# Row sums by float32 transposes, one spreading moved, and loads dealt out in a two-branch attention kernel with gradients

## The chip, the core and the metric

The kernel runs on one core of a Trainium2 chip. A core has five engines that run their own instruction queues: TensorE (matrix products and transposes into PSUM, the accumulators' memory), VectorE, ScalarE, GpSimd, and SyncE, which only issues DMAs. GpSimd and ScalarE issue DMAs too, in line with their other work. In the profile these are PE (with PEld for the loading of weights), DVE, ACT, POOL and SP. The metric is the device time of one execution, in microseconds (us).

## The reference

The forward pass mixes two branches token by token, `g * a + (1 - g) * b`, with a gate `g = sigmoid(sum(x * gate_w))`. There are 2048 tokens of width 576.

Branch a is attention with 32 query heads of width 18 and a single key and value head:

```python
q = (x @ wq).reshape(B, S, H, Dh).transpose(0, 2, 1, 3)
k = x @ wk
v = x @ wv
p = softmax(einsum('bhqd,bkd->bhqk', q, k) * Dh ** (-0.5))
a = einsum('bhqk,bkd->bhqd', p, v).transpose(0, 2, 1, 3).reshape(B, S, H * Dh) @ wo
```

Branch b goes through the tokens in 64 segments of 32, with 8 memory rows that each segment hands to the next:

```python
for s in range(n_seg):
    h = concatenate([mem, x[:, s * seg_len:(s + 1) * seg_len]], axis=1)
    q, k, v = (einsum('btd,dhe->bhte', h, W) for W in (Wq, Wk, Wv))
    scores = where(mask, einsum('bhqe,bhke->bhqk', q, k) * scale, -1e9)
    o = einsum('bhqk,bhke->bhqe', softmax(scores), v)
    o = einsum('bhte,hed->btd', o, Wo)
    mem = o[:, :M]
    outs.append(o[:, M:])
```

with 32 heads of width 128. The kernel returns the output and, for a given gradient of it, the gradients of `x`, of branch a's four weights, of the first memory, of branch b's four weights and of `gate_w`, twelve arrays in bfloat16.

## The kernel before

The program is one unrolled stream of instructions per engine; the order on each engine is the order in which the Python code writes it (most of it runs under a manual schedule). Its stages, one after another:

1. Preparation and the token projections of branch b.
2. The forward chain woven with pass 1 of branch a (from about 420 to 2147 us). The memory rows of branch b form a chain over 64 segments, `b_chain_fwd`; it yields 16 times a segment. `weave` takes one step of pass 1 (`a_pass1`, 1024 steps: the product `a_S`, its exponential `a_E`, the product `a_dP`, the elementwise `a_W`, the accumulations `a_acc`) and then one step of the chain, in turn. At the head of each segment but the first, the new memory rows are put together: the output projection of the segment before has left 32 x 4 partial rows in PSUM, VectorE has copied them to `c_hs` (line 565) and, masked, to `c_hx` (line 566), and `row_sums` adds the groups of rows and turns the result so that the model's width lies along the partitions: four float32 products with a 0/1 selector (`selp`, `sel8`). `put_rows` (line 322) copies the result to `hm`, the tile that the next projections load as weights. Helper lines 82 and 87 issue nearly all products and transposes.
3. The token stage `b_bulk` (from about 2160 to 2790 us): attention of the 2048 tokens of branch b, forward and backward, in 128 groups of 4 heads x 128 tokens. It is a pipeline written by hand: iteration `t` runs the stages of the list `order`, each for group `t - n`. `st_R` sums the exponentials of a row (`x_l`, line 816), takes the reciprocal (`x_r`) and lets GpSimd write `x_P`; `st_OT` transposes the attention output into the PSUM tile `x_tr`, of which there are two in turn, and VectorE copies it to `x_oT` (line 841); `st_VT` transposes `v` into the next `x_tr`; `st_T` and `st_DT` are VectorE transposes (`x_PT`, `x_DT`); `st_Y` is GpSimd's `x_Y` and `x_dS`. Four groups are one chunk, for which SyncE loads q, dO, k, v and the block-diagonal memory rows kB and vB; `after` says behind which stage of the chunk's last group each load for a later chunk is issued. Stores are collected in `due` and issued by `flush` at the end of a later iteration. q, dO and k have rings of four chunks; when the chunks run out, the same places load twelve weight tiles for the next stage.
4. The backward chain woven with pass 2 of branch a (from about 2814 to 4500 us): `b_chain_bwd`, 16 steps a segment, last segment first, each behind one step of `a_pass2` (`b_S`, `b_E`, `b_dP`, `b_dS`, `b_acc`). In 44 of the segments each segment also carries four units of other work, the memory rows' share of the keys' and values' gradients: `kv_load`, `kv_blk` (line 1085: GpSimd spreads a block of P or dS over four masked copies, `r_kb`), `kv_mm` (the products, into `r_x`) and `kv_out` (ScalarE copies to `r_kvo`, GpSimd issues the store, line 1109). `kv_mm(n)` also calls `kv_blk(n + 1)`. In the chain's own work, GpSimd copies `r_dS` into `r_dspad` (line 1039), VectorE transposes it to `r_dsq` (line 1043), GpSimd spreads that to `r_dSqB` (line 270), and TensorE uses it two steps later.
5. Post-processing, weight gradients and the final stage (from about 4500 us).

Of the kernel before, what the change touches and what calls it, by code (L numbers as in the profile page):

```python
# [10 lines left out]
ALU = mybir.AluOpType  # L11
AX = mybir.AxisListType
BF16 = mybir.dt.bfloat16
F32 = mybir.dt.float32
U16 = mybir.dt.uint16
U32 = mybir.dt.uint32
P = 128
# [3 lines left out]
NSL = 6  # L21
# [25 lines left out]
class Kern:  # L47
# [83 lines left out]
    def setup_B_consts(self, pool):  # L131
        nc = self.nc
# [40 lines left out]
        s8 = pool.tile([P, 8], F32, name="sel8")  # L173
        nc.gpsimd.memset(s8[:], 0.0)
        tm = pool.tile([P, 2, 32], BF16, name="tmask")
        nc.gpsimd.memset(tm[:], 0.0)
        sq = pool.tile([P, 2, 8], F32, name="selp")
        nc.gpsimd.memset(sq[:], 0.0)
        for c in range(4):
            nc.gpsimd.affine_select(out=s8[:], in_=s8[:], compare_op=ALU.not_equal, fill=1.0,  # L180
                                    base=-32 * c, pattern=[[-1, 8]], channel_multiplier=1)
            nc.gpsimd.affine_select(out=sq[:, c % 2, :], in_=sq[:, c % 2, :], compare_op=ALU.not_equal, fill=1.0,
                                    base=-32 * c, pattern=[[-1, 8]], channel_multiplier=1)
            nc.gpsimd.memset(tm[32 * c:32 * c + 32, c % 2, :], 1.0)
        self.sel8, self.selp = s8, sq
# [129 lines left out]
    def row_sums(self, pm, hs, hx):  # L315
        for k in range(2):
            self.mm(pm[:, 0:4, :].rearrange("p (f k) q -> p k f q", k=2)[:, k], lhsT=hs[:, k, :], rhs=self.selp[:])
        for j in range(2):
            self.mm(pm[:, 4 + j, :], lhsT=hx[:].rearrange("p a b -> p (a b)")[:, 64 - 64 * j:192 - 64 * j], rhs=self.sel8[:])

    def put_rows(self, t, pm):
        self.nc.vector.tensor_copy(t[:, :, 0:8], pm[:])
# [18 lines left out]
    def b_chain_fwd(self, keep, sp, psum):  # L341
# [69 lines left out]
        for s in range(NSEG):  # L411
# [43 lines left out]
            if s:  # L455
                pm = psum.tile([P, NSL, 8], F32, name="c_pj", bufs=1)
                self.row_sums(pm, hs, hx)
                self.put_rows(h_, pm)
# [208 lines left out]
    def b_bulk(self, wp, vp, kp, sp, psum):  # L667
# [65 lines left out]
        def flush(end=False):  # L733
            for dst, src in due.pop(0):
                (nc.scalar if end else nc.sync).dma_start(dst, src)
            due.append([])
# [169 lines left out]
        def st_KE(t):  # L906
# [3 lines left out]
            if t % 4 == 3:  # L910
                c2 = t // 4 % 2
                for i in range(4):
# [3 lines left out]
        order = [(2, st_M), (0, st_QT), (None, mem_T), (5, st_B0), (0, st_KT), (2, st_R), (4, st_Y), (5, st_B1), (4, st_OT),  # L916
                 (2, st_GT), (3, st_T), (5, st_DT), (3, st_Om), (5, st_Qm), (2, st_VT), (1, st_Sm), (3, st_Dm), (1, st_S),
                 (5, st_K), (3, st_D), (5, st_KE), (3, st_O), (5, st_Q)]
        after = {st_O: ("vB", "v"), st_D: ("mT",), st_KE: ("q", "dO"), st_Q: ("k", "kB")}
# [7 lines left out]
        for t in range(NG + 6):  # L927
            sc["D"] = psum.tile([P, 512], F32, name="x_D", bufs=1)
            sc["Sb"] = psum.tile([P, 512], F32, name="x_S", bufs=1)
            for n, st in order:  # L930
                if n is None:
                    st(t)
                    continue
                if 0 <= t - n < NG:
                    st(t - n)
                if st in after and t - n >= 0 and (t - n) % 4 == 3:
                    c = (t - n) // 4
                    for w in after[st]:
                        load(c + (BQ if w in deep else 3 if w in ("mT", "v") else 2), (w,))
            if t % 4 == 2 and t // 4 - 2 in range(NTT // 4):  # L940
                self.dl_rows(t // 4 - 2, sp, psum)
            flush(t >= NG)
        flush(True)
# [51 lines left out]
    def b_chain_bwd(self, wot, sp, kd, kvp, keep, psum):  # L995
# [93 lines left out]
        def kv_mm(n):  # L1089
# [10 lines left out]
            kv_blk(n + 1)  # L1100
# [19 lines left out]
        for s in reversed(range(NSEG)):  # L1120
# [81 lines left out]
            kv_mm(n0)  # L1202
# [7 lines left out]
            dSqB = blocks(dSq, "r_dSqB")  # L1210
            x_rows(s, 1, dS[:, 0, :])
# [1016 lines left out]
```

## Time and profile before

| | |
|---|---|
| median of 3 runs | 5489.96 us (5474.08 to 5496.04) |
| the profiled execution's own time | 5533.9 us |
| its span, first to last instruction | 5532.2 us |
| mean granted TensorE clock | 0.979 |
| busy: PE, PEld | 5142.1 us (93%), 2995.0 us (54%) |
| busy: DVE, ACT, POOL | 3602.5 (65%), 3331.9 (60%), 2405.3 us (43%) |
| 420 to 2147 us (forward chain, pass 1) | PE busy 1615.33 of 1727.00 us, DMA share 0.65 |
| 2160 to 2790 us (token stage) | PE busy 548.05 of 630.00 us, DMA share 0.74 |
| 2814 to 4500 us (backward chain, pass 2) | PE busy 1578.54 of 1686.00 us, DMA share 0.81 |

How to read the lines: a row of the timeline has the start in us from the span's start, the length in us, the engine, the line of the kernel, the operation, the tiles as out<-in, and how many like it run in a row (xN); in brackets, how long the engine had stood idle before it and what ended that. "issue" there means that the profile shows nothing that was waited for. A group has its busy time in us, the mean length of one in ns and the idle time ahead of it. A row of the waits has who waited for whom, the total in us, how many times, and the longest. A stretch has its bounds and length, the busy time (and number of instructions) of PE, PEld, DVE, ACT and POOL, the granted clock, the busy share of the 16 DMA engines and GB/s. A DMA queue has its packets, MB and share of the DMA engines; "q8 instruction" brings instructions in blocks of 16 KB.

### The profile page before, as it was taken

To read this page: it belongs to the slowest core of one execution; us is meant where nothing else is said; L and a number is where in the kernel's file an instruction comes from. 1 tells how busy PE (TensorE), PEld (TensorE's weight loads), DVE (VectorE), ACT (ScalarE), POOL (GpSimd) and SP (SyncE) were. 2 spreads that over 40 slices of the span, in tenths; PEclk is the share of its full clock that TensorE was granted. 3 is DMA by queue.
4 is the path that set the end of the run, shared out by engine and by line. 5 is a ranking of instruction groups with operands and counts; after the bars stand their busy time and mean duration, and the time that the engine had idled before them with its cause. 6 is when DMAs were issued, how large, how long until landed. Compare 5 with 4: busy or idle time off the path is not lost. (4 is left out here: it accounts for less than half of the span.)

```text
span 5532.2 us, 218543 instructions
## 1 busy us (share of the span) xinstructions
PE 5142.1 (93%) x93728; PEld 2995.0 (54%) x93728; DVE 3602.5 (65%) x7070; ACT 3331.9 (60%) x4816; POOL 2405.3 (43%) x4642
## 2 busy tenths in 40 slices
PE   7999999999999998888879999999998899999998
PEld 6435555555555555676635555555554457764444
DVE  5338888888878887666658888888888851121111
ACT  4327777787778876555557787787877752111101
POOL 4004555555555544433335666666653421122223
PEclk9999999999999999999979999999999999999999
DMA  6646677676676556777775898888886679986653
GB/s 214 229 178 136 132 133 132 136 138 131 135 130 125 112 104 159 223 220 226 223 225 146 185 199 189 190 191 195 191 177 142 140 158 227 240 234 225 201 173 108
DMA packets 1118177, 961.48 MB, mean 174 GB/s; under 512 B 692275, under 2 KB 944700, under 8 KB 1107603
## 3 DMA queue, kind: packets, MB, share of 16 engines
q1 hardware_dynamic: 1012578, 701.92, 55.2%
q0 software_dynamic: 100016, 242.38, 15.0%
q8 instruction: 733, 12.01, 1.0%
q10 hardware_dynamic: 4608, 3.20, 0.2%
q14 instruction: 242, 1.97, 0.1%
HBM read 521.16 MB, written 357.96 MB: 159 GB/s over the span
## 5 line engine op out<-in xcount | busy, mean ns | idle before, releaser
L1801 DVE TENSOR_TENSOR a_W<-a_dP,a_E 128x512 bf16<-128x512 f32 x2048 | 1314.2, 683 | 281.3 <-issue 118.6
L1947 DVE TENSOR_TENSOR b_dS<-b_dP,b_E 128x512 bf16<-128x512 f32 x2048 | 1307.0, 682 | 237.0 <-issue 98.4
L1924 ACT ACTIVATE b_E<-b_S 128x1024 bf16<-128x1024 f32 x1024 | 1049.1, 1025 | 285.1 <-PE b_dP L82 214.6
L1768 ACT ACTIVATE a_E<-a_S 128x1024 bf16<-128x1024 f32 x1024 | 1050.1, 1025 | 268.7 <-PE a_dP L82 195.1
L82 PEld LDWEIGHTS <-b_QS 32*128 32x128 bf16 (+1 forms) x8192 | 268.8, 92 | 568.0 <-issue 521.3
L82 PE MATMUL r_pj<-WT,r_dT 128*32 128x288 bf16 x12288 | 500.7, 287 | 4.0 <-issue 4.0
L82 PE MATMUL b_S<-b_KV,b_QS 32*128 32x512 bf16 x2048 | 404.7, 384 | 88.2 <-ACT b_E L1924 64.9
L82 PE MATMUL w_acc<-w_d,w_h 128*128 128x512 bf16 (+1 forms) x2400 | 473.8, 379 | 0.0
L82 PE MATMUL a_S<-a_QD,l_KV 32*128 32x512 bf16 x2048 | 403.7, 385 | 54.5 <-ACT a_E L1768 37.5
L82 PE MATMUL b_acc<-b_dS,b_QS 128*32 128x512 bf16 x2048 | 436.7, 393 | 2.2 <-DVE b_dS L1947 1.4
L82 PE MATMUL a_acc<-a_E,l_VK 128*32 128x256 bf16 x8192 | 407.4, 275 | 19.6 <-issue 14.6
L82 PE MATMUL b_dP<-b_KV,b_QS 32*128 32x512 bf16 x2048 | 418.1, 389 | 7.4 <-DVE b_dS L1947 1.4
L82 PE MATMUL b_acc<-b_E,b_QS 128*32 128x512 bf16 x2048 | 407.2, 394 | 0.2
L82 PE MATMUL a_dP<-a_QD,l_KV 32*128 32x512 bf16 x2048 | 402.4, 389 | 1.1 <-DVE a_W L1801 1.0
L82 PEld LDWEIGHTS <-r_dT 128*32 128x32 bf16 x12288 | 335.4, 97 | 95.6 <-issue 7.4
L82 PEld LDWEIGHTS <-w_h 128*128 128x128 bf16 (+1 forms) x2688 | 229.8, 100 | 258.4 <-issue 6.6
L82 PE MATMUL a_acc<-a_W,l_WK 128*32 128x256 bf16 x4096 | 306.1, 284 | 4.2 <-issue 3.6
L82 PEld LDWEIGHTS <-l_KV 32*128 32x128 bf16 x4096 | 147.9, 91 | 292.3 <-issue 269.5
L79 ACT CAST w_o<-w_acc 128x512 bf16<-128x512 f32 x54 | 31.7, 586 | 384.3 <-PE w_acc L82 376.0
L77 DVE CAST w_o<-w_acc 128x512 bf16<-128x512 f32 x54 | 37.3, 692 | 333.4 <-PE w_acc L82 306.5
L82 PEld LDWEIGHTS <-l_VK 128*32 128x32 bf16 x8192 | 220.5, 97 | 42.5 <-issue 35.9
L82 PEld LDWEIGHTS <-hm 128*32 128x32 bf16 x7680 | 202.7, 97 | 74.8 <-issue 6.3
(465 smaller groups left out, 10701.1 us busy)
## 6 DMA issues: line engine op xcount, KB each, us to landing
b_QS<-qs_dram SPq DMA_DIRECT2D x256, 256.0 KB
dOx_dram<-p_tok SPq DMA_DIRECT2D x16, 1024.0 KB
c_vx<-vx_dram SPq DMA_DIRECT2D x64, 256.0 KB
krow_dram<-c_k POOLq DMA_DIRECT2D x64, 256.0 KB
qrow_dram<-c_q POOLq DMA_DIRECT2D x64, 256.0 KB
vrow_dram<-c_v POOLq DMA_DIRECT2D x64, 256.0 KB
x_q<-qx_dram SPq DMA_DIRECT2D x32, 512.0 KB
x_k<-kx_dram SPq DMA_DIRECT2D x32, 512.0 KB
```

Source lines behind the costliest of these rows:

```text
L77: nc.vector.tensor_copy(out, in_)
L79: nc.scalar.copy(out, in_)
L82: return self.nc.tensor.matmul(out, lhsT, rhs, start=start, stop=stop, tile_position=tp, skip_group_check=True)
L1768: nc.scalar.activation(E_[n][:], S.pop(n)[:], ACT.Exp, scale=SCALEA)
L1801: nc.vector.tensor_tensor(out=W_[n][:, i, :], in0=dP[i][:], in1=E_[n][:, i, :], op=ALU.mult)
L1924: nc.scalar.activation(E_[n][:], S.pop(n)[:], ACT.Exp, scale=SCALEA)
L1947: nc.vector.tensor_tensor(out=D_[n][:, i, :], in0=dP[i][:], in1=E_[n][:, i, :], op=ALU.mult)
```

## The change

Three edits that do not depend on each other.

Forward: `row_sums` no longer multiplies by selectors. It transposes the two halves of `c_hs` and the two halves of `c_hx` in float32 (128 x 128 each, with the identity `identF`) into one PSUM tile of a whole bank, and two VectorE reductions add the groups out of it, of two and of four values, writing `hm` directly. The selectors and `put_rows` go.

```diff
-    def row_sums(self, pm, hs, hx):
+    def row_sums(self, h, hs, hx, psum):
+        nc = self.nc
+        pm = psum.tile([P, 4, P], F32, name="c_pj", bufs=1)
         for k in range(2):
-            self.mm(pm[:, 0:4, :].rearrange("p (f k) q -> p k f q", k=2)[:, k], lhsT=hs[:, k, :], rhs=self.selp[:])
+            nc.tensor.transpose(pm[:, k, :], hs[:, k, :], self.identF[:])
         for j in range(2):
-            self.mm(pm[:, 4 + j, :], lhsT=hx[:].rearrange("p a b -> p (a b)")[:, 64 - 64 * j:192 - 64 * j], rhs=self.sel8[:])
-
-    def put_rows(self, t, pm):
-        self.nc.vector.tensor_copy(t[:, :, 0:8], pm[:])
+            nc.tensor.transpose(pm[:, 2 + j, :], hx[:].rearrange("p a b -> p (a b)")[:, 64 - 64 * j:192 - 64 * j],
+                                self.identF[:])
+        with nc.allow_low_precision(reason="sums of two and four float32 values, rounded once"):
+            nc.vector.tensor_reduce(out=h[:, 0:4, 0:8].rearrange("p (f k) q -> p f k q", k=2),
+                                    in_=pm[:, 0:2, :].rearrange("p k (c f q) -> p f k q c", c=2, f=2)[:, :, :, 0:8, :],
+                                    axis=AX.X, op=ALU.add)
+            nc.vector.tensor_reduce(out=h[:, 4:6, 0:8], in_=pm[:, 2:4, :].rearrange("p j (g q) -> p j q g", g=4)[:, :, 0:8, :],
+                                    axis=AX.X, op=ALU.add)
...
             if s:
-                pm = psum.tile([P, NSL, 8], F32, name="c_pj", bufs=1)
-                self.row_sums(pm, hs, hx)
-                self.put_rows(h_, pm)
+                self.row_sums(h_, hs, hx, psum)
```

Token stage: `st_R` runs behind `st_OT` instead of ahead of `st_Y`. The load of dO is issued one iteration later than before and that of k three iterations later, at the end of the iteration, ahead of the stores; kB is issued where k was.

```diff
-        order = [(2, st_M), (0, st_QT), (None, mem_T), (5, st_B0), (0, st_KT), (2, st_R), (4, st_Y), (5, st_B1), (4, st_OT),
-                 (2, st_GT), (3, st_T), (5, st_DT), (3, st_Om), (5, st_Qm), (2, st_VT), (1, st_Sm), (3, st_Dm), (1, st_S),
+        order = [(2, st_M), (0, st_QT), (None, mem_T), (5, st_B0), (0, st_KT), (4, st_Y), (5, st_B1), (4, st_OT),
+                 (2, st_R), (2, st_GT), (3, st_T), (5, st_DT), (3, st_Om), (5, st_Qm), (2, st_VT), (1, st_Sm), (3, st_Dm), (1, st_S),
                  (5, st_K), (3, st_D), (5, st_KE), (3, st_O), (5, st_Q)]
-        after = {st_O: ("vB", "v"), st_D: ("mT",), st_KE: ("q", "dO"), st_Q: ("k", "kB")}
+        after = {st_O: (("vB", 0), ("v", 0)), st_D: (("mT", 0),), st_KE: (("q", 0), ("dO", 1)), st_Q: (("kB", 0), ("k", 3))}
+        later = {}
...
-                    for w in after[st]:
-                        load(c + (BQ if w in deep else 3 if w in ("mT", "v") else 2), (w,))
+                    for w, wait in after[st]:
+                        later.setdefault(t + wait, []).append((c + (BQ if w in deep else 3 if w in ("mT", "v") else 2), (w,)))
+                        if wait == 0:
+                            load(*later[t].pop())
             if t % 4 == 2 and t // 4 - 2 in range(NTT // 4):
                 self.dl_rows(t // 4 - 2, sp, psum)
+            for x in later.pop(t, ()):
+                load(*x)
             flush(t >= NG)
+        for t in sorted(later):
+            for x in later[t]:
+                load(*x)
         flush(True)
```

Backward: the first of a segment's four spreadings is no longer issued inside `kv_mm(n0)` but one step of the chain later, behind `r_dSqB`.

```diff
-        def kv_mm(n):
+        def kv_mm(n, blk=True):
...
-            kv_blk(n + 1)
+            if blk:
+                kv_blk(n + 1)
...
             heads(2)
-            kv_mm(n0)
+            kv_mm(n0, False)
...
             dSq = pad_T("ds")
             dSqB = blocks(dSq, "r_dSqB")
+            if n0 >= 0:
+                kv_blk(n0 + 1)
             x_rows(s, 1, dS[:, 0, :])
```

More of the change, by code (lines that the diff above doesn't have):

```diff
@@ L172, in setup_B_consts @@
         self.seln = sn
-        s8 = pool.tile([P, 8], F32, name="sel8")
-        nc.gpsimd.memset(s8[:], 0.0)
         tm = pool.tile([P, 2, 32], BF16, name="tmask")
         nc.gpsimd.memset(tm[:], 0.0)
-        sq = pool.tile([P, 2, 8], F32, name="selp")
-        nc.gpsimd.memset(sq[:], 0.0)
         for c in range(4):
[L180 to L183, printed above, removed]
             nc.gpsimd.memset(tm[32 * c:32 * c + 32, c % 2, :], 1.0)
-        self.sel8, self.selp = s8, sq
         self.tmask = tm
```

## The prediction

> **What bounds the kernel now.** I read the busy shares first, then a table of stretches, then single iterations in the timeline, then the waits and the DMA queues of those places.
>
> ```profile
> PE 5142.1 (93%) x93728; PEld 2995.0 (54%) x93728; DVE 3602.5 (65%) x7070; ACT 3331.9 (60%) x4816; POOL 2405.3 (43%) x4642
> ```
>
> TensorE is the engine to watch; a change elsewhere counts only where TensorE waits for it. Stretches of the token stage and of the backward chain (length, busy time by engine, then granted clock, DMA share, GB/s), then four stretches of the token stage, each from one exponential of the scores to the next, one iteration:
>
> ```profile
> 2160.00:2790.00 630.00, 548.05 (x14129) 435.37 (x14128) 419.85 (x1412) 362.34 (x771) 252.56 (x405) 0.95 0.74 221
> 2814.00:4500.00 1686.00, 1578.54 (x32848) 833.36 (x32848) 1399.33 (x2427) 1309.69 (x1709) 938.14 (x1565) 0.98 0.81 178
> ```
> ```profile
> 2472.80:2476.94 4.14, 4.14 (x122) 3.31 (x120) 3.22 (x11) 2.81 (x8) 1.92 (x4) 1.00 0.90 273
> ...
> 2481.24:2487.65 6.41, 4.18 (x120) 3.33 (x112) 3.22 (x11) 2.91 (x7) 2.54 (x4) 1.00 0.69 202
> 2487.65:2493.24 5.59, 5.59 (x132) 4.37 (x120) 3.43 (x11) 2.81 (x7) 1.33 (x3) 0.69 0.85 235
> ```
> ```profile
> L804 ACT ACTIVATE x_E<-x_S x128: 384/389/402, 2161.9 to 2787.8; 128x256 bf16<-128x256 f32 x128
> ```
>
> A clean iteration takes 4.14 us and TensorE fills it. The third stretch does the same work (4.18 busy) in 6.41, and the next is slow because the granted clock fell to 0.69 behind the gap. From the last row, 127 iterations take 625.9 us, 4.93 each: 100 us above the clean rate (625.9 - 127 x 4.14). That excess is what the third part of the change can touch. What ends the gap:
>
> ```profile
> 2487.05 0.17 PEld L82 LDWEIGHTS <-x_dOT 128*128 128x128 bf16 x4 [2.33 <-issue]
> ```
> ```profile
> q8 instruction: 1, 0.02, 2.6%
> ```
> ```profile
> q1 hardware_dynamic: 1317, 1.54, 87.8%
> ...
> x_k<-kx_dram SPq DMA_DIRECT2D x1, 512.0 KB
> ```
> ```profile
> PEld L82 <- issue: 60.9, 42, 3.3
> ```
>
> The gap of 2.33 us waits for no tile and no engine ("issue"). The second fence is the DMA view of the gap itself (2484.7 to 2487.0): the instruction queue lands one block. The third is the same view of the 5.7 us before it (2479.0 to 2484.7): no instruction block at all, the data queue holding 87.8% of the DMA engines with the k load and what SyncE issues behind it (kB and the stores of dS and dm, by the order in the code). So TensorE's instructions run out while their fetch queues behind data. The last row is the waits view of 2240 to 2800: 42 such gaps, 60.9 us, under the weight loads of one line alone.
>
> **The change, part by part.** All counts are from the listing of the instruction order: TensorE has as many instructions as before and the same order throughout, VectorE 63 more, the DMAs are the same in number.
>
> *Forward memory rows (63 segments).* Four float32 products with a selector go, each of two passes; four float32 transposes come, and two VectorE sums take the place of one copy.
>
> ```profile
> 1074.48 0.53 PEld L82 LDWEIGHTS c_pj<-selp,c_hs 128*128 128x128 f32 x4
> ...
> 1075.47 0.10 PEld L82 LDWEIGHTS <-l_KV 32*128 32x128 bf16 x4
> ...
> 1075.58 0.21 DVE L322 CAST hm<-c_pj 128x48 bf16<-128x48 f32 x1 [0.49 <-PE c_pj L82]
> ...
> 1076.03 0.22 PEld L82 LDWEIGHTS <-hm 128*32 128x32 bf16 x8
> ...
> 1076.67 0.20 PEld L1839 LDWEIGHTS c_x<-identF,a_acs 128*128 128x128 f32 x2 [0.42 <-issue]
> ...
> 1077.04 0.10 PEld L82 LDWEIGHTS <-l_KV 32*128 32x128 bf16 x4 [0.17 <-issue]
> ```
> ```profile
> L1839 PE MATMUL c_x<-identF,a_acs 128*128 128x128 f32 x252 | 55.1, 300 | 0.0
> ...
> L566 DVE TENSOR_TENSOR c_hx<-c_pj,tmask 128x64 f32<-128x64 f32 x63 | 13.4, 212 | 0.0
> ```
> ```profile
> L816 DVE TENSOR_REDUCE x_l<-x_E x128: 406/409/410, 2163.2 to 2789.1; 128x4 f32<-128x256 bf16 x128
> ```
>
> The sums hold TensorE from 1074.48 to 1075.47, 0.99 us, with the sweep's next product right behind. Two transposes of this form, already in the kernel, take 0.37 (1076.67 to 1077.04), four 0.74: gain 0.25. By the group's busy time (55.1 / 252 = 0.22 each) four take 0.88: gain 0.11. I take the middle, 0.18, times 63: -11 us (ends -16 and -7). On VectorE the nearest row to a sum over 64 float32 values out of PSUM is the 64-element one, 0.212; the far one is the 256-element sum, 0.409. Two at 0.21 instead of the copy's 0.21 add 0.21; starting 0.18 sooner they end 0.03 later than the copy did (1075.79, now 1075.82), and TensorE wants the rows 0.18 sooner than 1076.03, at 1075.85: just hidden. If that cover goes (0.41 each: end at 1076.22), TensorE stands 0.37 a segment, +23 us, net +12. I take the near row because the cost goes with elements in these rows (212 for 64, 409 for 256). The selector constants that vanish are nine GpSimd instructions of the set-up; nothing waits for them there: 0.
>
> *Backward spreading (44 segments).* The spreading of P or dS (r_kb) moves from ahead of the copy r_dspad to behind the spreading r_dSqB on GpSimd. Waits of 2980 to 4160, then the timeline of one segment:
>
> ```profile
> DVE r_dsq L1043 <- POOL r_dspad L1039: 30.1, 41, 1.5
> ```
> ```profile
> 3354.18 1.07 POOL L1085 TENSOR_TENSOR r_kb<-r_ks,bmask 128x512 bf16<-128x512 bf16 x1
> 3355.20 0.23 POOL L1039 COPY r_dspad<-r_dS 128x64 bf16<-128x64 bf16 x1
> 3355.37 0.61 POOL L1109 DMA_DIRECT2D dvx_dram<-r_kvo  x1
> 3356.00 0.65 POOL L270 TENSOR_TENSOR r_dSqB<-r_dsq,bmask 128x256 bf16<-128x256 bf16 x1
> ```
> ```profile
> 3354.33 0.58 ACT L1108 CAST r_kvo<-r_x 128x512 bf16<-128x512 f32 x1
> ...
> 3355.46 0.45 DVE L1043 STREAM_TRANSPOSE r_dsq<-r_dspad 128x256 bf16<-128x256 bf16 x1 [0.72 <-POOL r_dspad L1039]
> ...
> 3356.13 0.39 PE L82 MATMUL b_S<-b_KV,b_QS 32*128 32x512 bf16 x2
> ...
> 3356.96 0.10 PEld L82 LDWEIGHTS <-b_QS 128*32 128x32 bf16 x2 [0.73 <-issue]
> ...
> 3357.99 0.18 PE L82 MATMUL r_x<-r_dSqB,r_q 128*128 128x32 bf16 x1
> ...
> 3358.45 0.39 PE L82 MATMUL b_S<-b_KV,b_QS 32*128 32x512 bf16 x2
> ...
> 3359.35 0.23 PEld L82 LDWEIGHTS <-r_kb 128*128 128x128 bf16 x4 [0.24 <-issue]
> ```
> ```profile
> 4146.03 0.39 PE L82 MATMUL b_S<-b_KV,b_QS 32*128 32x512 bf16 x2
> 4147.58 0.39 PE L82 MATMUL b_S<-b_KV,b_QS 32*128 32x512 bf16 x2
> ```
>
> VectorE stands 0.72 us with the sweep's products queued behind r_dsq, and TensorE then stands 0.73: this step takes 2.32 (3356.13 to 3358.45). The same step of a segment that has no spreading left takes 1.55 (the last two rows). The difference, 0.77, is on the path; 41 waits make -31 us (44 would be -34). New waits: the r_dvx store's issue on GpSimd waits for ScalarE's r_kvo (done 3354.91), and r_dSqB stands behind it; 3354.91 + 0.61 + 0.65 = 3356.17, wanted at 3357.99 less 0.77: a second to spare. Then r_kb ends at 3357.24 and is wanted at 3359.35 less 0.77. The r_xq store behind it is an issue on GpSimd that no one awaits within the segment. If the second to spare goes, the 31 us go with it.
>
> *Token stage, row sums.* VectorE's x_l and x_r move behind the copy x_oT; the multiplication x_P on GpSimd moves behind x_Y and x_dS.
>
> ```profile
> 2480.38 0.27 DVE L746 STREAM_TRANSPOSE x_DT<-x_dS 128x128 bf16<-128x128 bf16 x1
> ...
> 2481.44 0.39 PE L82 MATMUL x_po<-x_k,x_DT 32*32 32x128 bf16 x16
> ...
> 2483.31 0.39 PE L87 MATMUL x_tr<-identB,x_o 128*128 128x128 bf16 x4
> ...
> 2483.90 0.39 DVE L841 COPY x_oT<-x_tr 128x512 bf16<-128x512 bf16 x1
> ...
> 2484.35 0.21 PEld L87 LDWEIGHTS <-x_v 128*128 128x128 bf16 x3 [0.28 <-issue]
> ```
>
> The v transposes take the buffer that this copy frees, and stand 0.28. The copy could start at 2483.70 instead of 2483.90: 0.20 a clean iteration, taken for half of the 127 (in the others the fetch decides): -12 us (ends 0 and -25). What gets later is x_DT, by 0.39; it has 0.79 before its use (2480.65 to 2481.44): hidden. GpSimd, busy 1.92 of 4.14, hides the moved multiplication.
>
> *Token stage, loads.* One chunk is four iterations. dO is issued one iteration later, k three, kB now ahead of k; the last weight load falls behind the loop. On SyncE's queue the stores of dS, dm and dq move up past them. k keeps five iterations of 4.1 us before its use, against 512 KB at 221 GB/s, 2.4 us: hidden. Two of the three loads leave the place where the fetch starves. Ends: 0, and the whole excess less the 12 above, about -90. The nearest row for evenly spread traffic is the backward chain: DMA share 0.81, more than the 0.74 here, yet TensorE is busy 94%. That argues for the far end; that the stores stay bunched, and that a shorter stage raises the share towards 0.83, argues against. I take half of the excess: -50 us.
>
> The Trainium skill, page "Runtime: NRT & Kernel Launch", section "Instruction fetch mechanics", says that crossing a 16 KiB block is mostly hidden, instructions being dispatched more slowly than the memory fills. By it this last edit is worth 0 and the sum ends 50 us higher. The fences on the fetch above speak against it.
>
> **Sum.** -11 - 31 - 12 - 50 = -104 us on the profiled execution's 5533.9. That execution stands 44 us above the median 5489.96; some of these 44 may be the same gaps. Taken from the median: 5386; I say 5390.
>
> **Rivals.**
> The loads buy nothing: the fetch is late wherever they stand. For it: the stores' share of the traffic is unchanged. Against: clean iterations exist at a share of 0.90. Time: 5390 + 50 = 5440. (The rule of the Trainium skill quoted above would end at the same time.)
> The backward wait comes back behind r_kvo: no gain there, 5421. Against: the slack of a second.
> The forward sums come late (0.41 each): 5413. Against: the 64-element row.
> Slower: spread loads delay the fetch in all four iterations of a chunk instead of two. At the mean of the two slow ones, (6.41 + 5.59) / 2 = 6.00, the stage takes 762 us, +136; with the other terms (-54) +82: 5572. It decides once the stage's mean iteration passes 4.93 + 54 / 127 = 5.36. Against: the mean share is 0.74.
>
> **How the numbers follow.** Forecast 0.50 (its own range 5340 to 5425), loads nothing 0.22, backward wait 0.10, late sums 0.10, slower 0.08. The range 5330 to 5465 reaches from the far end of the loads to the loads at nothing with one small loss more; only the slower rival is left out. A measurement of this kernel tells 0.5%, 27 us, from no change (the three runs differ by 22). All cases but the last are below 5462 alone; combined they reach it: faster 0.87, same 0.06, slower 0.07.
>
> **What would show it.** Right: step between two b_S at r_dsq down to 1.55; r_dsq no longer waiting for r_dspad; the 42 gaps under "issue" in the token stage halved, its length near 565; the row-sum step 0.15 to 0.2 shorter, r_hm weights not waiting for VectorE. Wrong: gaps of the same sum at other iterations, or TensorE waiting for r_dSqB or for the sums.

## The result, and the profile after

| | before | after |
|---|---|---|
| median of 8 runs each | 5496.91 us (5474.08 to 5513.43) | 5441.34 us (5431.47 to 5462.47) |
| ratio after / before | | 0.9904, 95% interval 0.9883 to 0.9925 |
| the profiled execution's own time | 5533.9 us | 5450.0 us |
| forward chain and pass 1, first to last `a_S` | 1727.9 us | 1706.4 us |
| token stage, first to last `x_E` | 625.9 us | 593.7 us |
| backward chain and pass 2, first to last `b_S` | 1683.8 us | 1657.2 us |

The kernel is faster by 56 us by the medians, and by 53 (0.96%) by the ratio. Forecast were 104 us, and 5390 us as the time. The time lies in the range that was given, the gain is half of the forecast.

The first row of the page after (busy time and share by engine), and the three stages in the view of stretches (length, busy time of PE, PEld, DVE, ACT, POOL, granted clock, DMA share, GB/s):

```profile
PE 5055.0 (93%) x93298; PEld 2951.0 (54%) x93476; DVE 3625.4 (67%) x7133; ACT 3329.4 (61%) x4816; POOL 2408.8 (44%) x4632
```
```profile
419.20:2125.60 1706.40, 1591.55 (x35098) 871.96 (x35097) 1427.69 (x2553) 1361.56 (x1787) 900.48 (x2087) 0.99 0.65 130
2139.80:2733.50 593.70, 516.60 (x13953) 428.13 (x14044) 425.93 (x1403) 359.21 (x767) 255.76 (x402) 0.96 0.79 234
2759.90:4417.10 1657.20, 1548.44 (x32808) 825.53 (x32809) 1400.01 (x2425) 1308.28 (x1708) 937.62 (x1563) 0.99 0.82 181
```

TensorE still bounds the kernel (93%). In the token stage the DMA share rose from 0.74 to 0.79 and the rate from 221 to 234 GB/s: the same bytes in less time.

**Forward.** The timeline after, around the row sums of one segment:

```profile
1066.70 0.25 PEld L310 LDWEIGHTS c_pj<-identF,c_hs 128*128 128x128 f32 x2
1066.81 0.38 PE L310 MATMUL c_pj<-identF,c_hs 128*128 128x128 f32 x2
1066.92 0.25 PEld L312 LDWEIGHTS c_pj<-identF,c_hx 128*128 128x128 f32 x2
1067.03 0.38 PE L312 MATMUL c_pj<-identF,c_hx 128*128 128x128 f32 x2
1067.34 0.10 PEld L82 LDWEIGHTS <-l_KV 32*128 32x128 bf16 x4 [0.17 <-issue]
...
1067.45 0.23 DVE L315 TENSOR_REDUCE hm<-c_pj 128x32 bf16<-128x64 f32 x1
1067.59 0.21 DVE L318 TENSOR_REDUCE hm<-c_pj 128x16 bf16<-128x64 f32 x1
```

The four transposes hold TensorE from 1066.70 to 1067.34, 0.64 us, where the selector products held it 0.99. The step (one `a_S` to the next) fell from 2.30 to 1.94 us in every segment; the step behind it is unchanged at 1.57, so the sums are not late. Over 63 segments that would be 22 us.

**Backward.** The timeline after, around the spreading that was moved:

```profile
3290.08 0.39 PE L82 MATMUL b_S<-b_KV,b_QS 32*128 32x512 bf16 x2
3290.15 0.43 DVE L1046 STREAM_TRANSPOSE r_dsq<-r_dspad 128x256 bf16<-128x256 bf16 x1
...
3290.70 0.61 POOL L1113 DMA_DIRECT2D dvx_dram<-r_kvo  x1 [0.81 <-ACT r_kvo L1112]
3291.32 0.65 POOL L261 TENSOR_TENSOR r_dSqB<-r_dsq,bmask 128x256 bf16<-128x256 bf16 x1
3291.63 0.39 PE L82 MATMUL b_S<-b_KV,b_QS 32*128 32x512 bf16 x2
3291.91 1.08 POOL L1088 TENSOR_TENSOR r_kb<-r_ks,bmask 128x512 bf16<-128x512 bf16 x1
3292.70 0.18 PE L82 MATMUL r_x<-r_dSqB,r_q 128*128 128x32 bf16 x1
```

`r_dsq` no longer waits, and the step takes 1.55 us (3290.08 to 3291.63) instead of 2.32. GpSimd waits 0.81 for ScalarE's `r_kvo` before the store, as the prediction had it, and `r_dSqB` still ends (3291.97) 0.7 us before its use.

**Token stage.** A clean iteration after, in the view of stretches; then a gap in the timeline, and the DMA queues in the gap (2439.3 to 2441.6) and in the 6.2 us before it (2433.0 to 2439.2):

```profile
2251.73:2255.66 3.93, 3.88 (x122) 3.30 (x120) 3.32 (x11) 2.81 (x8) 1.97 (x4) 1.00 0.84 253
```
```profile
2441.69 0.10 PEld L82 LDWEIGHTS <-x_oT 128*128 128x128 bf16 x1 [2.70 <-issue]
```
```profile
q1 hardware_dynamic: 957, 0.50, 78.0%
q8 instruction: 1, 0.02, 2.5%
```
```profile
q1 hardware_dynamic: 944, 1.65, 87.4%
```

The clean iteration is 0.21 us shorter (4.14 before). The gaps are still there and look the same: an instruction block lands in the gap, none in the 6 us before, while the data queue holds 87% of the DMA engines. The waits under the weight loads of line 82 in the whole stage, first before, then after:

```profile
PEld L82 <- issue: 64.6, 45, 3.3
```
```profile
PEld L82 <- issue: 51.2, 36, 2.9
```

Taken over both of TensorE's queues (idle stretches over 0.3 us between the first and the last `x_E`, summed up from the trace), 75.8 us in 49 gaps became 66.0 us in 46. By the iteration of the chunk (t mod 4 = 0, 1, 2, 3) they were 9.9, 38.4, 23.1 and 4.5 us, and are 20.0, 22.7, 14.3 and 9.0: the gaps went to other iterations, and few went away.

### The profile page after: what moved, and what is told of

The parts are those of the page before. It is cut to its first block, busy times and chain, and to the rows that moved or that the text cites. A ratio compares the mean times of both kernels' runs of the same rounds, so it can differ in the third digit from the quotient of the medians.

```text
span 5448.3 us, 218047 instructions
## 1 busy us (share of the span) xinstructions
PE 5055.0 (93%) x93298; PEld 2951.0 (54%) x93476; DVE 3625.4 (67%) x7133; ACT 3329.4 (61%) x4816; POOL 2408.8 (44%) x4632
## 4 chain that ended last, share of the span: by engine, by line
PE 52%; issue 8%; ACT 6%; POOL 3%; DMA 3%; DVE 0%; SPq 0%; POOLq 0%; ACTq 0%; DVEq 0%
PE w_acc L82 12%; PE r_pj L82 7%; PE b_S L82 6%; PE b_acc L82 5%; PE r_x L82 5%; ACT b_E L1930 4%; PE x_tr L87 3%; PE x_b L82 2%; PE x_po L82 2%; PE a_acc L82 2%; PE a_S L82 2%; PE c_pj L82 1%; PE c_x L82 1%; ACT a_E L1774 1%; DMA b_QS<-qs_dram 1%
## 5 line engine op out<-in xcount | busy, mean ns | idle before, releaser
L82 PE MATMUL b_acc<-b_dS,b_QS 128*32 128x512 bf16 x2048 | 425.0, 393 | 0.2
L82 PE MATMUL b_dP<-b_KV,b_QS 32*128 32x512 bf16 x2048 | 402.8, 388 | 0.2 <-DVE b_dS L1953 0.2
L1088 POOL TENSOR_TENSOR r_kb<-r_ks,bmask 128x512 bf16<-128x512 bf16 x176 | 188.6, 1072 | 126.9 <-DMA r_ks<-px_dram 45.3
```

The costliest lines, as they stand in the source:

```text
L82: return self.nc.tensor.matmul(out, lhsT, rhs, start=start, stop=stop, tile_position=tp, skip_group_check=True)
L1088: nc.gpsimd.tensor_tensor(out=B[:], in0=a[:].unsqueeze(2).to_broadcast([P, 4, 4, SEG]), in1=self.bmask[:, :, 0].unsqueeze(1).unsqueeze(3). ...
```

## The experiments

Below, "late fetches" are those idle stretches over 0.3 us that end under "issue" between 1.0 and 1.9 us after an instruction block has landed; "gaps" are all over 0.3 us. Stage lengths are measured as in the table above. One execution is profiled per kernel, and the token stage varies: 625.9, 615.7, 606.5 and 621.3 us in the four kernels here that leave it as it was (before, e1, e2, e14). The profiled executions of e2, e3, e7 and e11 are the fastest of their kernels' runs and those of before and e14 the slowest, so a difference of 10 us between the stages of two kernels shows little; the ratios go by all runs.

A gap also costs more than its length. In the clock record of the token stage before, the granted clock falls to 0.5 twelve times, for 3.41 us each, each time within 1.5 us of the end of a gap of 1.5 to 3.1 us: 41.0 us in all, and 34.1 after. At half the clock TensorE loses about half of that time, by estimate 20 us before and 17 after; this is called the clock loss below.

### The parts one by one

From the kernel before, e1 takes the forward part of the diff alone, e2 the backward part, e3 the order of the token stage, e4 its loads.

```diff
# e3_rows: the order alone
-        order = [(2, st_M), (0, st_QT), (None, mem_T), (5, st_B0), (0, st_KT), (2, st_R), (4, st_Y), (5, st_B1), (4, st_OT),
-                 (2, st_GT), ...
+        order = [(2, st_M), (0, st_QT), (None, mem_T), (5, st_B0), (0, st_KT), (4, st_Y), (5, st_B1), (4, st_OT),
+                 (2, st_R), (2, st_GT), ...
# e4_loads: the loads alone (with `later`)
-        after = {st_O: ("vB", "v"), st_D: ("mT",), st_KE: ("q", "dO"), st_Q: ("k", "kB")}
+        after = {st_O: (("vB", 0), ("v", 0)), st_D: (("mT", 0),), st_KE: (("q", 0), ("dO", 1)), st_Q: (("kB", 0), ("k", 3))}
```

> The kernel before with the forward edit alone (four float32 transposes and two VectorE sums in place of four selector products and a copy). By the prediction's term: 11 us less than before. By the two traces (the row-sum step 2.30 us before, 1.94 after, 63 segments): 22 us less, the row-sum step at 1.94. If the work only moves to the steps behind it: 0, with the next steps longer by what this step loses.

> The kernel before with the backward edit alone (the first spreading of a segment moved behind r_dSqB). By the prediction's term: 31 us less. By the two traces (the whole backward chain 27 us shorter): 27 us less, the step at r_dsq down from a median of 2.32 to 1.55 in 41 to 44 segments, the other steps a few us longer in sum. If the stall returns behind r_kvo: 0.

> The kernel before with the row sums of the token stage moved behind the copy x_oT, loads as before. By the prediction's term, which counts half of the iterations: 12 us less. If every iteration is 0.20 shorter, the stalled ones too: 25 us less, token stage near 601. If the instruction fetch sets the pace in the stalled iterations and a shorter iteration leaves it less time: the gaps grow by what the clean iterations gain, and the gain is 0 to 12.

> The kernel before with the loads of the token stage dealt out (dO one iteration later, k three, kB ahead of k), row sums as before. By the prediction's term: 50 us less, the 42 gaps under the weight loads of the token stage halved (60.9 to 30 us), the stage near 576 us. By the rival that the fetch is late wherever the loads stand: 0 (within 6 us), the same sum of gaps at other iterations, the stage near 620. By a third view, that spreading the loads shortens the fetch's best places: slower by some 10 us.

| | ratio to before, 95% interval | us | forward | token | backward |
|---|---|---|---|---|---|
| e1_fwd | 0.9985 (0.9971 to 0.9999) | -8 | 1707.4 | 615.7 | 1673.2 |
| e2_bwd | 0.9971 (0.9957 to 0.9986) | -16 | 1716.1 | 606.5 | 1656.1 |
| e3_rows | 0.9991 (0.9976 to 1.0007) | -5 | 1712.5 | 595.9 | 1673.1 |
| e4_loads | 0.9964 (0.9949 to 0.9979) | -20 | 1715.0 | 590.1 | 1677.5 |

The four add up to -49 us, the whole change measures -53 by its ratio: the ratios show no part helping or hindering another. (The token stage of e3, e4 and after, 595.9, 590.1 and 593.7 us in one execution each, leaves open how far the two edits there add up.) None reaches its term except, within its interval, the forward sums and the row sums. The loads bring 20 of 50 us. The stage of e4 in the view of stretches and its waits under line 82:

```profile
2149.00:2739.00 590.00, 527.48 (x13954) 423.44 (x14044) 416.61 (x1403) 359.54 (x767) 250.86 (x401) 0.97 0.80 235
```
```profile
PEld L82 <- issue: 41.3, 42, 2.9
```

The gaps are as many (42 here, 45 before) and a third shorter in sum; they moved from iterations 1 and 2 (38.4 and 23.1 us) to 0 and 1 (19.3 and 17.9). Iterations 1 and 2 lost 33 us of gaps, 0 and 3 gained 9; in the kernel after it is 25 and 15. So the loads clear a place in part, and a part comes back beside it.

Profiles of the same stage in several kernels say where the rest went. The forward chain averages 1717.9 us in the four kernels without the forward edit (before, e2, e3, e4) and 1710.2 in the nine with it (after, e1, e5 to e10, e13; 1704.6 to 1715.9): 8 us, though the step is 22 us shorter in each. The backward chain averages 1676.7 us in five kernels without its edit (before, e1, e3, e4, e14) and 1657.8 in nine with it (after, e2, e5, e6, e8 to e11, e13): 19 us, though the step at `r_dsq` is 31 us shorter (133 to 102.5 us, summed over the segments in the same kernels). The expectation of e7 below has 35 for it: that is a mean over the middle segments, in most of which there is a spreading, taken for all. In both chains other steps got longer by the difference.

### The loads undone

```diff
# e10_undo, from the kernel after
-        after = {st_O: (("vB", 0), ("v", 0)), st_D: (("mT", 0),), st_KE: (("q", 0), ("dO", 1)), st_Q: (("kB", 0), ("k", 3))}
+        after = {st_O: ("vB", "v"), st_D: ("mT",), st_KE: ("q", "dO"), st_Q: ("k", "kB")}
```

> The changed kernel with the loads where they were before. By the prediction's term the loads are worth 50 us: ratio to before 0.9995 (5494). By the run with the loads alone (0.9964 of before, stage some 26 us shorter): 20 us, ratio 0.994. If the loads are worth something only as long as the row sums are slow (the changed kernel's stage, 594, is no shorter than that of either edit alone, 596 and 590): 0, ratio 0.9904, stage at 594.

Ratio 0.9943 (0.9924 to 0.9963), token stage 604.9 us, gaps 66.6 us. Against 0.9904 of the whole change, the loads are worth 21 us (5 to 37 by the two intervals), as in e4. The price of 20 us stands from both sides; that they are worth nothing once the row sums are fast is refuted by the ratios. The gaps, though, have the same sum as in the kernel after (66.6 and 66.0 us); what differs in the two executions is the clock loss, 27 us against 17, and it varies as much between kernels with the same stage (12 to 20 us in before, e1, e2 and e14).

### Does the fetch wait behind data?

e5 thins the large loads, e6 leaves out the small ones. Both leave data stale, so that their outputs are not the reference's.

```diff
# e5_thin, from the kernel after
+                    n = 32 if k in old else P      # k in old: this buffer has been filled once
-                    nc.sync.dma_start(d[w].rearrange("p h e -> p (h e)"),
-                                      self.xtok[w][tt * P:(tt + 1) * P, h0 * P:h0 * P + 2048])
+                    nc.sync.dma_start(d[w][0:n].rearrange("p h e -> p (h e)"),
+                                      self.xtok[w][tt * P:tt * P + n, h0 * P:h0 * P + 2048])
# e6_small, from the kernel after
+                    if c % 2 == 0 and tt >= 2:
+                        mT[tt] = mT[tt - 2]
-                    for i in range(4):
+                    for i in range(4 if c < 2 else 0):
```

> The changed kernel, in which the loads of q, dO, k and v in the token stage bring 32 of the 128 partitions once their buffers have been filled (1.5 MB of some 4.3 MB a chunk less, all in 4-KB packets; places and number of the loads as in the changed kernel; the rest of the tile keeps older data, so the output is not the reference's). If TensorE runs dry because the fetch of its instructions stands behind data: the DMA share falls from 0.79 to about 0.45, the gaps from 66 us to under 20, the stage from 594 to about 520 us. If the fetch is late by itself: the gaps stay within 10 us of 66 and the stage at 594.

> The changed kernel without the loads of kB, vB and the transposed memory rows (mT) behind the first of each buffer: 0.5 MB a chunk less, in 1024 packets of 256 B and 512 of 512 B, a third of all packets but 11% of the DMA engines' time; their issues on SyncE go too (some 5 us of 16 a chunk). Output not the reference's. If the fetch stands behind the time of the data: gaps some 10 to 15 us less, the stage at 575 to 585. If it stands behind the number of packets or of issues: a third of the gaps or more goes, 25 us or more, the stage under 570.

The stage of e5 and then of e6 in the view of stretches, each with its waits under line 82:

```profile
2150.40:2675.50 525.10, 502.90 (x14053) 418.48 (x14054) 424.68 (x1403) 358.04 (x768) 255.88 (x402) 0.98 0.61 180
```
```profile
PEld L82 <- issue: 11.4, 16, 1.8
```
```profile
2145.50:2748.30 602.80, 531.79 (x14054) 435.16 (x14055) 426.77 (x1403) 362.14 (x768) 256.75 (x402) 0.94 0.67 205
```
```profile
PEld L82 <- issue: 60.4, 40, 3.1
```

Without three quarters of the large loads the stage takes 525 us, 69 less, the gaps fall from 66.0 to 16.5 us (the late fetches from 56.4 to 8.7), the clock is never at half in the stage, and 4.13 us an iteration is all that is left (clean: 3.93); the ratio to before is 0.9781 (0.9747 to 0.9814, two runs). So the late fetch is caused by data traffic, that of the large loads; this is shown, and it settles the rival that blocks come late by themselves. In the prediction, the Trainium skill (page "Runtime: NRT & Kernel Launch", section "Instruction fetch mechanics") was quoted with the rule that crossing a block is mostly hidden: e5 comes near to it (16.5 us of gaps in 525), the kernel after does not (66.0 in 594).

e6 came out as neither theory had it: two fifths of the packets less (the DMA view of 2200 to 2670 has 63,877, after has 106,262), a share of 0.67, and the same gaps, 66.0 us, 33.4 of them in iteration 1 and 24.1 in iteration 0. The loads that are left run closer together: by half iterations the DMA share goes from 0.22 to 0.99, where it goes from 0.66 to 0.88 after. Neither the number of packets nor the mean share tells how late the fetch is. With fewer bytes e6 is even slower than the kernel after: ratio 0.9951 (0.9934 to 0.9968) against 0.9904, 26 us. The profiled executions differ by 19: 9 in the token stage, where the clock loss is 26 us against 17, and 5 in each chain.

### Long transfers, or their places?

```diff
# e8_half, from the kernel after: loads of q, dO, k, v and stores of o, dq in halves of 64 partitions, two iterations apart
+                        for i in range(2):
+                            later.setdefault(t + wait + 2 * i, []).append(x + (i,))
+                    for i in range(2):
+                        due[1 + 2 * i].append((dst[...64 * i...], src[64 * i:64 * i + 64]...))
# e13_halfload: the same for the loads, stores whole
# e9_bunch, from the kernel after
-        after = {st_O: (("vB", 0), ("v", 0)), st_D: (("mT", 0),), st_KE: (("q", 0), ("dO", 1)), st_Q: (("kB", 0), ("k", 3))}
+        after = {st_D: (("mT", 0),), st_Q: (("vB", 0), ("v", 0), ("q", 0), ("dO", 0), ("kB", 0), ("k", 0))}
```

> The changed kernel, in which each 512-KB transfer of the token stage (loads of q, dO, k, v, stores of o and dq) goes in two halves of 64 partitions, two iterations apart; same bytes and packets, six issues a chunk more on SyncE (some 2.4 of 16 us, on a queue that is some 85% taken). If the fetch is late because it stands behind a long transfer, in the stretches where the DMA engines are full: gaps from 66 to some 35 us, the stage from 594 to about 560, 0.006 below the changed kernel's ratio. If only the total of the traffic counts: gaps and stage as in the changed kernel (within 10 us). If SyncE's queue is full by the six issues: transfers late, the stage over 610.

> The changed kernel with the loads of q, dO, k and v in two halves of 64 partitions, two iterations apart, the stores whole again (four issues a chunk more on SyncE, some 2 of 16 us). The run with halved loads and stores had few late fetches (11.5 us against 56) but TensorE stood 70 us for kB and for the buffer of x_dq. If halves help the fetch and only the halved stores hurt: fetch gaps under 35 us, the stage about 570. If the fetches were only on time there because TensorE stood for the data: gaps and stage as in the changed kernel (594, within 10 us). If the four issues already fill SyncE's queue: TensorE waits for kB again, the stage over 605.

> The changed kernel with the loads of vB, v, q, dO, kB and k of a chunk all issued in one place, the last stage of its fourth iteration; same bytes and packets. If the fetch is late in the stretches where the DMA engines are full: gaps over 85 us instead of 66, most of them in the two iterations behind that place, the stage over 610 instead of 594. If only the total counts: gaps and stage as in the changed kernel (within 10 us).

| | ratio to before, 95% interval | runs | token stage | late fetches | other gaps | clock loss |
|---|---|---|---|---|---|---|
| after | 0.9904 (0.9883 to 0.9925) | 8 | 593.7 | 56.4 us (43) | 9.6 us (3) | 17 us |
| e8_half | 0.9982 (0.9967 to 0.9997) | 12 | 635.6 | 11.5 us (13) | 92.2 us (33) | 34 us |
| e13_halfload | 0.9904 (0.9869 to 0.9940) | 2 | 593.4 | 35.4 us (33) | 37.8 us (28) | 9 us |
| e9_bunch | 0.9871 (0.9837 to 0.9905) | 2 | 570.3 | 44.3 us (36) | 8.3 us (3) | 3 us |

The waits of e8 in 2141.0 to 2776.6, and of e13 in its token stage:

```profile
PE x_po L82 <- ACT x_dq L771: 78.4, 27, 5.9
PEld L87 <- DMA x_kmB<-km_dram: 74.8, 23, 5.9
ACT x_dq L771 <- DMA dqx_dram<-x_dq: 69.8, 18, 6.4
```
```profile
PE x_tr L87 <- DMA x_k<-kx_dram: 25.3, 14, 5.4
```

With halved transfers fewer fetches are late, and TensorE waits for data instead: in e8 for kB and for the buffer of `x_dq`, whose store lands two iterations later, in e13 for k, whose second half is issued two iterations later than the whole was. All gaps together are 73.2 us in e13 and 66.0 after. So it is not shown that halves help the fetch: a fetch may be in time only because TensorE stands for the data anyway, and a stage of 593 us is what the expectation names for that case. e9 refutes that a crowd of loads makes things worse: with all loads of a chunk in one place the gaps are 52.6 us, most of them in the two iterations behind it (21.8 and 24.8), and the stage is shorter than in any other kernel here that does the whole work, but for e12 below. Against after it has 13 us less in gaps and, by the estimate, 14 us less clock loss. The time of the whole kernel differs from after by less than the intervals can tell. What is shown is that the traffic of the large loads causes the late fetches and that rearranging it moves them; which feature of the traffic sets their sum stays open.

### What takes the backward gain back

```diff
# e7_qs4, from the kernel after
-                QS = sp.tile([P, 2, 512], BF16, name="b_QS", bufs=3)
+                QS = sp.tile([P, 2, 512], BF16, name="b_QS", bufs=4)
-                    load(n // 4 + 2)
+                    load(n // 4 + 3)
-            xq = sp.tile([P, 2, 32], BF16, name=f"r_xq{x}", bufs=1)
+            xq = sp.tile([P, 2, 32], BF16, name="r_xq", bufs=1)
```

> The changed kernel with b_QS of the backward chain loaded one chunk further ahead (four buffers for three; r_xq0 and r_xq1 share one buffer to make the room). The backward edit shortened its step by 0.55 us a segment (35 us) and the whole chain only by 20; the traces show TensorE waiting for the landing of b_QS 8 to 12 times more often than before, at steps 7 and 11 of a segment. If these late loads are what takes the gain back: steps 7 and 11 return to 1.56 to 1.64, the chain is 8 to 12 us shorter than in the changed kernel (1657 to about 1647), the ratio to before some 0.002 lower than 0.9904. If they are only the sign of a full DMA system: another load is late in their place, the chain within 3 us of 1657.

The waits of the weight loads for `b_QS` in the backward chain: before, after, and in e7.

```profile
PEld L82 <- DMA b_QS<-qs_dram: 22.9, 8, 9.1
```
```profile
PEld L82 <- DMA b_QS<-qs_dram: 38.5, 25, 10.6
```
```profile
PEld L82 <- DMA b_QS<-qs_dram: 12.5, 4, 10.1
```

Each row has one wait of 9 to 11 us for the first load of the stage. With the chain faster, the load of `b_QS` lands late 25 times instead of 8. Loaded a chunk earlier it does so 4 times, and the chain takes 1642.2 us, 15 less than after and 34.5 less than the mean without the edit, where the step at `r_dsq` saves 31. So in this execution the late loads of `b_QS` took back all of the 12 us that were missing. In e12 below, which has the same edit, `b_QS` is late 3 times and the chain takes 1650.9, 7 less than the mean with the backward edit: one load further ahead brings 15 us in one execution and 7 in the other, around the 12 that were missing. On the whole kernel it is not resolved: ratio 0.9899 (0.9874 to 0.9924), median 5441.99.

### What takes the forward gain back

By segment (mean lengths of segments 4 to 59), the forward edit makes three kinds shorter and one longer: s mod 4 = 0, 1, 2, 3 take 28.1, 26.8, 26.2 and 26.3 us without it (before, e2, e3, e4), and 28.5, 26.4, 26.0 and 26.0 with it (after, e1, e7 to e10, e13). In the first kind GpSimd issues a zero fill of 512 KB for `pq`.

```diff
# e11_zero4 from the kernel after, e14_zero_before from the kernel before
-            if s % 4 == 0:
-                nc.gpsimd.dma_start(self.pq_dram[s // 4]...rearrange("p (n z) -> p n z", z=256), z4[:].unsqueeze(1).to_broadcast([P, 8, 256]))
+            zr = slice(32 * (s % 4), 32 * (s % 4) + 32)
+            nc.gpsimd.dma_start(self.pq_dram[s // 4]...rearrange("p (n z) -> p n z", z=256)[zr], z4[zr].unsqueeze(1).to_broadcast([32, 8, 256]))
```

> The changed kernel with the zero fill of pq in the forward chain (512 KB on GpSimd's DMA queue in every fourth segment) dealt into four quarters, one a segment. In all runs so far these fourth segments take 28.3 us where the others take 26.0 to 26.4, and the forward edit, which makes the other three kinds 0.2 to 0.4 us shorter, leaves them 0.4 us longer. If the fill is what makes TensorE's instructions late there: the fourth segments fall to about 26.5, the forward chain from 1706 to about 1680, the ratio to before from 0.9904 to about 0.986. If it is another transfer of the fourth segment (the store of c_oh, issued at the end of the segment before): the fourth segments stay at 28.3, the chain within 8 us of 1706.

> The kernel before with the zero fill in quarters and nothing else. Together with the changed kernel with quarters this gives the forward edit's worth where the fill does not stand in its way. If the fourth segments took the edit's gain back because of the fill: this kernel's forward chain is 18 us or more longer than that of the changed kernel with quarters (the edit's 22 us come through), where with the whole fill the means of the runs differ by 8. If the gain is lost in another way: the two chains differ by 8 us again. Against before itself: about 25 us less, ratio 0.9955, if the fill is to blame; 0 if not.

e11: ratio 0.9906 (0.9885 to 0.9928), chain 1705.1 us; the four kinds take 27.4, 27.2, 26.0 and 26.0. e14: 0.9970 (0.9953 to 0.9988), chain 1716.0 us. The fourth segments lose 0.9 us and the next ones gain 0.8: the gaps went along with the fill, their sum stayed (late fetches 39.8 us in e11, 36.9 after). The edit is worth 11 us with the fill dealt out (1716.0 less 1705.1, one execution each, the slowest of its runs and the fastest), not 22. For the changed kernel my theory of the fill has fallen. In the kernel before, the fill in quarters makes the time 16 us less by the ratio, which the theory (25) is not far from, but the chain in the profiled execution is only 2 us shorter than the mean, so where the 16 us come from stays open. Of the 14 us of the forward gain that come back, about half are late fetches (37.2 us in the mean of the nine kernels with the edit, 30.8 in the four without); the other half are waits for ScalarE's `a_E` (11.6 and 7.8 us) and for GpSimd's `c_PBx` (6.1 and 2.7). Which transfer makes the fetches late stays open. The other candidate, the store of `c_oh`, wasn't tried and stands.

### Together

e12 is the kernel after with the edits of e7, e9 and e11.

> The changed kernel with three things together: the zero fill in quarters, b_QS a chunk further ahead, and the token stage's loads of a chunk all issued in one place. By the sum of the terms as the traces have them (forward 25, backward 15, token stage 24 us): 64 us under the changed kernel, ratio about 0.979. If what one stage gains is lost elsewhere: no better than the best of the three alone, 0.987.

Ratio 0.9835 (0.9812 to 0.9857), median 5410.5 us: the fastest version, 38 us below the kernel after by the ratios. Its stages, in the view of stretches and by the first and last `b_S` (2728.0 to 4378.9), are 1694.8, 569.8 and 1650.9 us, together 42 less than after; the token stage:

```profile
2130.90:2700.70 569.80, 511.98 (x13951) 425.38 (x14043) 425.45 (x1403) 359.48 (x767) 255.22 (x398) 0.97 0.79 244
```

That is two thirds of the 64 us that were expected, but the forward term of 25 in that sum had not come in e11 either (1 us). What the single edits brought in their traces, 1 in the forward chain (e11), 23 in the token stage (e9) and 15 in the backward chain (e7), adds up to some 40, and 42 came, as 12, 24 and 6: the edits don't take from each other by anything that these executions resolve. The DMA system now moves 244 GB/s in the token stage where it moved 234, with 47.7 us of gaps instead of 66.0.

## Why the prediction was wrong

The steps that the forward and backward edits and the row sums shorten were seen rightly; what the loads do to the fetch was not, and that was half of the sum. The ratios of the four parts fall 55 us short of the forecast (49 against 104): 30 with the loads, 15 backward, 7 with the row sums, 3 forward. By the stages' means, 8 us came from the forward chain, 19 from the backward chain and 28 from the token stage (617.4 in the four kernels without an edit there, 589.6 in after, e7 and e11): 55, against 56 by the medians. Forecast were 11, 31 and 62.

*Loads: the step that failed.* "Two of the three loads leave the place where the fetch starves ... I take half of the excess: -50 us." They are worth 20 (e4) and 21 (e10). The sentence treats the starved fetch as a matter of place. The traces show the gaps in other iterations after the move: 25 us left the two old places and 15 came up in the other two. e5 shows that it is a matter of traffic, since the gaps go with the bytes of the large loads; e9 that another order moves the gaps. That is most of the prediction's own sign of being wrong ("gaps of the same sum at other iterations"): the sum fell from 72 to 63 us in the means of the kernels named above, the clock loss from 17 to 15. The rest of the 28 us of this stage, some 18 by difference, goes with the shorter iteration. Its near row, the backward chain with a share of 0.81 and TensorE at 94%, was no argument: at 0.61 to 0.67 in e5 and e6 the gaps are 16.5 and 66.0 us, so the share does not tell how late the fetch is. And the excess of 100 us was read from an execution that was slow in just this stage: 625.9 us, where the mean of four is 617.4, which leaves 92.

*Backward: the right step and the wrong sum.* The step saves 31 us as forecast, no wait came back behind `r_kvo`, and the second of slack held. The chain gains 19 and the kernel 16. The working asked who waits on GpSimd's queue; it did not ask what else was only just in time for the sweep. `b_QS`, loaded by SyncE two chunks ahead, was next: late 25 times instead of 8 (e7).

*Forward: two errors that cancel.* The prediction took the middle of two estimates for the transposes, a gain of 0.18 us a segment; it is 0.36, since four in a row hold TensorE for 0.64 us, 0.16 each; the pair from which 0.37 was read must hold a start that is paid once, as two more cost only 0.27. That makes 22 us, of which 14 come back as longer steps. The 8 us measured agree with the forecast of 11 by chance. VectorE's two sums take 0.23 and 0.21 us, as the near row said, and are not late. That TensorE has as many instructions as before holds for the code; in the profile each selector product loads its weights twice and each transpose once, 252 weight loads fewer in all (93,728 and 93,476).

*Row sums.* The clean iteration went from 4.14 to 3.93 us: 0.20 was forecast. Taken for half of the iterations, 12 us; e3 gives 5, with an interval from a gain of 13 to a loss of 4, and 17 by the stages' means (600.4 in e3 and e10 against 617.4). The shorter iteration came as forecast; the time that it brings is not contradicted, and e3 alone does not tell it from nothing.

*The rivals.* "The loads buy nothing" gave 5440, and 5441 was measured, but not for its reason: the loads bring 20 us, and the backward chain lacks 15. The slower rival had no part in it: the mean iteration after is 4.67 us (593.7 / 127), below its 5.36.

## What to carry to other kernels

An edit that shortens a step on the bound engine is worth what the whole stage gains, not what the step does: here two fifths and two thirds came back in the two chains. Where this was followed up, the same bytes then had to move in less time and the next transfer, an operand or a block of instructions, was late. So ask which loads are only just in time at today's pace, and give them one more buffer along with the edit. When an engine starves for instructions under heavy traffic, don't price a new order of the loads by the place that they leave: the gaps can come up at the next. Only fewer bytes in large loads made them go here (e5); fewer small ones did not (e6), and the order that was expected to be worst had fewer gaps than that of the change (e9, 52.6 us against 66.0, one execution each). Count the clock behind a gap with the gap, and read such a stage's excess from more than one execution.

## What the runs showed of the hardware

- Late instruction blocks come from the traffic of the large loads: 66.0 us of gaps at 234 GB/s and 16.5 at 180 (e5), with the same instructions. The rate by itself does not tell: 66.0 us at 205 GB/s in e6, 47.7 at 244 in e12. All 43 gaps under "issue" after ended 1.2 to 1.7 us after a 16-KB block had landed and 2.2 to 2.8 us after it began to move (the gap that ends at 2441.69: 1.45 and 2.38), though they are 0.4 to 2.8 us long; what varies is when the block begins.
- Behind 12 gaps of 1.5 to 3.1 us in the token stage before, the granted clock was 0.5 for 3.41 us.
- Leaving out two fifths of the packets, all of them small, left the gaps at 66.0 us (e6), though the DMA share fell from 0.79 to 0.67.
- With the loads of 512 KB in two halves, two iterations apart, late fetches were 35 us instead of 56 and waits for data came in their place (e13); the stage stayed at 593 us.
- Float32 transposes of 128 x 128 take 0.16 us each in a row of four; VectorE adds 64 float32 values a row out of PSUM in 0.21 to 0.23 us.
